# Linear attention and MLP on one core: the first chunk in halves of its heads, and loads and casts of the start moved

## The chip, the cores and the metric

The kernel runs on one core of a Trainium2 chip. The metric is the device time of one execution in microseconds (us). The engines are TensorE (PE; its weight loads are PEld), VectorE (DVE), ScalarE (ACT), GpSimd (POOL) and SyncE (SP), which here issues the loads. Each works through its own instructions in order and waits for the others by semaphores.

## The reference

Eight batches, eight heads, 576 positions, head size 64. First a linear attention, then an MLP over its output:

```
phi(x) = where(x > 0, x, exp(x) - 1) + 1
kv  = einsum(bhsd,bhse->bhde)(phi(k), v);  z = sum_s phi(k)
x   = einsum(bhsd,bhde->bhse)(phi(q), kv) / (phi(q) . z + 1e-6)   -> [4608, 512]
out = gelu_tanh(x @ w_in) @ w_out          w_in [512, 2048], w_out [2048, 512]
```

All inputs and the output are float32; the kernel multiplies in bfloat16.

## The kernel before

Everything is written out in program order by hand (`manual_schedule`); the order in the Python code is the order of each engine's instructions. The MLP runs in nine iterations (`iteration(j)`): iteration j takes the first 512 positions of batch j as four chunks of 128 tokens, and the ninth takes what is left of all batches. In an iteration h = x @ w_in is made in 16 blocks of 128 columns (`h_ps`, one PSUM bank each, four matmuls of 512 tokens, line 349), ACT applies GELU to each (line 359), and the second product (`o_ps`, line 650) accumulates over the 16 blocks for the four chunks. Work for later batches is hung onto the steps of an iteration by number with `at(j, slot, fn)`; in iteration 0 slots 0 to 15 are the h blocks and slots 16 to 31 are the groups of four o matmuls, in the order u (four blocks of w_out each) and, within it, chunk t.

PSUM is used as two pools: six single banks (`bank`, tag b) and one pair of banks (`pair_of_banks`). The loads of q, k, v, w_in and w_out share seven SBUF buffers (`pld`), and SP issues them in the order of the code: q and k of batch 0 in alternating halves, v in halves, four blocks of w_in (1 MB each), then w_out blocks between the loads of batch 1. Each w block is cast from float32 to bfloat16 by `cast_w_in` (line 137) or `cast_w_out` (line 143), which take the engine as an argument.

`first_batch` has nothing to overlap with. It makes phi of q and k (lines 212, 223, 236), transposes q on PE (line 395), casts v (line 241), makes kv in two halves `ii` (line 263; half ii gives the head pairs, or blocks, ii and 2+ii) and puts it as blocks into `kvbd` (line 290). `keep_warm(n)` issues n matmuls of zeros (line 385). Then for each chunk c: `nab` multiplies q by the four blocks (`n_ps`, line 294, in the pair of banks; `nab_in_banks` uses two single banks and evacuates them one by one), DVE divides (a reciprocal, lines 307 and 329, and a product, lines 309 and 330) into x; `transpose_x` transposes x by four PE matmuls into one bank (line 341), which ACT copies into xt (line 342). `h_quarter(0, c, 3)` computes h blocks 0 to 2 for that chunk alone, contracting over the four blocks of x's columns. Iteration 0 then goes on with the GELUs and blocks 3 to 15.

`plan_second` is the attention of batch 1, placed into iteration 0: `maps` (exp, linear part, minimum; slot 15), `transpose_q` (23), `casts` of v (25), `kv` and `last_w_out` (26), then `n` and `t` for the chunks (27 to 31). `gelu_table()` loads ACT's table with GELU; the exps need another table, and the framework inserts that load itself. Copies on ACT need neither.

Of the kernel before, what the change touches and what calls it, by code (L numbers as in the profile page):

```python
# [8 lines left out]
FP32 = mybir.dt.float32  # L9
BF16 = mybir.dt.bfloat16  # L10
# [5 lines left out]
def kernel(  # L16
# [57 lines left out]
    def bank(name, shape, dt=FP32):  # L74
        return ps_b.tile(shape, dt, name=name, tag="b")
# [51 lines left out]

    w_st = {}

    def load_w(wr, i):  # L130
        t = pld.tile([P, 4, 512], FP32, name="w_st", tag="ld")
        w_st[wr is w_in_r, i] = t
        src = wr[:, :, 512 * i : 512 * (i + 1)] if wr is w_in_r else wr[:, 4 * i : 4 * i + 4, :]
        nc.sync.dma_start(out=t, in_=src)

    def cast_w_in(i, fn, fs=slice(0, 512)):
        fn(
            out=w_in_sb[:, :, 512 * i + fs.start : 512 * i + fs.stop],
            in_=w_st[True, i][:, :, fs],
        )  # L140

    def cast_w_out(i, fn, ms=slice(0, 4)):
        fn(
            out=w_out_sb[:, 4 * i + ms.start : 4 * i + ms.stop, :],
            in_=w_st[False, i][:, ms],
        )
# [8 lines left out]
    for s in range(2):  # L155
        load_pairs("v", v, 0, halves[s])
    for i in range(4):
        load_w(w_in_r, i)
    load_w(w_out_r, 0)
    ld_tile("q", 1)  # L160
    load_q_paired(1)
# [95 lines left out]
    def kv_paired(b, ii, kv_of):  # L257
        kp, vp = phi["k", b], vp_paired(b)
        for j in range(J):
            for s in range(2):  # L260
                for a in range(2):
                    r, u = slice(HP * a, HP * (a + 1)), 2 * ii + s
                    nc.tensor.matmul(  # L263
                        kv_of(a, ii)[HP * s : HP * (s + 1)],
                        lhsT=kp[r, j, u, :],
                        rhs=vp[r, j, u, :],
                        start=(j == 0),
                        stop=(j == J - 1),
                        skip_group_check=True,
                    )  # L270
# [16 lines left out]
    def kv_evac(b, blocks, src, fn):  # L287
        for s in range(2):
            r = slice(HP * s, HP * (s + 1))
            fn(out=kvbds[b % 4][r, blocks, E * s : E * (s + 1)], in_=src[r])  # L290
# [44 lines left out]
            )  # L335
        return x

    def transpose_x(x, xt_c, fn):
        t_ps = bank("t_ps", [P, NP, P], BF16)
        for i in range(NP):  # L340
            nc.tensor.transpose(t_ps[:, i, :], x[:, P * i : P * (i + 1)], ident)  # L341
        fn(out=xt_c, in_=t_ps)

    xts = {}
    qts = {}

    def h_mm(h_ps, xt, m, ts=slice(0, MAIN)):
        for c in range(KM):
            nc.tensor.matmul(  # L349
                h_ps[:, ts],  # L350
                lhsT=w_in_sb[:, c, P * m : P * (m + 1)],
                rhs=xt[:, c, ts],
                start=(c == 0),
                stop=(c == KM - 1),
                skip_group_check=True,
            )
# [3 lines left out]

    h_begun = {0: {}, 1: {}}

    def h_begin(j, m, ts):
        if m not in h_begun[j]:
            h_begun[j][m] = bank("h_ps", [P, MAIN])
        h_mm(h_begun[j][m], xts[j], m, ts)

    def h_quarter(j, c, blocks):
        for m in range(blocks):
            h_begin(j, m, slice(P * c, P * (c + 1)))  # L370

    def xt_chunk(j, c):
        return xts[j][:, :, P * c : P * (c + 1)]
# [1 line left out]
    def gelu_table():  # L375
        nc.scalar.preload_act_table_set("gelu_apprx_tanh_and_others")  # L376
# [3 lines left out]
    def first_batch():  # L380
        w_ps = bank("w_ps", [P, 512])

        def keep_warm(n):
            for _ in range(n):
                nc.tensor.matmul(w_ps, lhsT=warm[:, 0:P], rhs=warm)  # L385

        qt = pt.tile([P, C, NP, P], BF16, name="qt")
        qs = (slice(0, 4), slice(4, 8))

        def transpose_q(s, fn):  # L390
            t_ps = bank("t_ps", [P, C, 2, P], BF16)
            for i in range(2):
                for c in range(C):
                    h = 4 * s + 2 * i
                    nc.tensor.transpose(
                        t_ps[:, c, i, :], phi["q", 0][:, c, h : h + 2, :], ident
                    )
            fn(out=qt[:, :, 2 * s : 2 * s + 2, :], in_=t_ps)

        keep_warm(18)  # L400
        for s in range(2):
            for n, hs in (("q", qs[s]), ("k", halves[s])):
                exp_of(n, 0, hs)
                linear_of(n, 0, hs)
                least_of(n, 0, hs)
        transpose_q(0, nc.scalar.copy)
        keep_warm(10)
        transpose_q(1, nc.scalar.copy)
        keep_warm(2)
        for ii in range(2):  # L410
            cast_v_paired(0, halves[ii], nc.vector.tensor_copy)
        for ii in range(2):
            kv_ps = [bank("kv_ps", [P, E]) for _ in range(2)]
            kv_paired(0, ii, lambda a, ii: kv_ps[a])
            for a, fn in enumerate((nc.vector.tensor_copy, nc.scalar.copy)):
                block = slice(2 * a + ii, 2 * a + ii + 1)
                kv_evac(0, block, kv_ps[a].rearrange("p (i e) -> p i e", i=1), fn)
        gelu_table()
        for s in range(2):
            cast_w_in(0, nc.gpsimd.tensor_copy, slice(256 * s, 256 * s + 256))  # L420
        for i in range(1, 4):
            cast_w_in(i, nc.gpsimd.tensor_copy)
        for i in range(2):
            cast_w_out(i, nc.gpsimd.tensor_copy)
        cast_w_out(2, nc.gpsimd.tensor_copy, slice(0, 2))
        keep_warm(2)

        xts[0] = pt.tile([P, NP, MAIN], BF16, name="xt")
        x = {0: nab(qt[:, 0], 0), 1: nab_in_banks(qt[:, 1], 0)}
        for c in range(C):  # L430
            transpose_x(x[c], xt_chunk(0, c), nc.scalar.copy)
            if c + 2 < C:
                x[c + 2] = (nab, nab_in_banks)[c % 2](qt[:, c + 2], 0)
            if c > 0:
                h_quarter(0, c - 1, 3)
        h_quarter(0, C - 1, 3)

    first_batch()

# [14 lines left out]
    def plan_second():  # L454
        b = 1
        x = {}

        def maps():
            for n in "qk":
                exp_of(n, b)  # L460
            gelu_table()
            for n in "qk":
                linear_of(n, b)
            least_of("q", b)
            cast_w_out(2, nc.vector.tensor_copy, slice(2, 4))
            least_of("k", b)

        def transpose_q():
            qts[b] = pt.tile([P, C, NP, P], BF16, name="qt")
            for s in range(2):  # L470
                t_ps = bank("t_ps", [P, 2, NP, P], BF16)
                for c in range(2):
                    for i in range(NP):
                        nc.tensor.transpose(  # L474
                            t_ps[:, c, i, :],
                            phi["q", b][:, 2 * s + c, 2 * i : 2 * i + 2, :],
                            ident,
                        )
                nc.scalar.copy(qts[b][:, 2 * s : 2 * s + 2], t_ps)

        def casts():
            cast_v_paired(b, halves[0], nc.vector.tensor_copy)
            cast_v_paired(b, halves[1], nc.gpsimd.tensor_copy)

        def kv():
            kv_ps = [bank("kv_ps", [P, 2, E]) for _ in range(2)]
            for ii in range(2):
                kv_paired(b, ii, lambda a, ii: kv_ps[a][:, ii, :])
            for a, fn in enumerate((nc.vector.tensor_copy, nc.scalar.copy)):
                kv_evac(b, slice(2 * a, 2 * a + 2), kv_ps[a], fn)  # L490

        def last_w_out():
            cast_w_out(3, nc.vector.tensor_copy, slice(0, 1))
            cast_w_out(3, nc.scalar.copy, slice(1, 2))
            cast_w_out(3, nc.gpsimd.tensor_copy, slice(2, 4))

        def n(c):
            x[c] = (nab_in_banks if c == 1 else nab)(qts[b][:, c], b)

        def t(c):  # L500
            if c == 0:
                xts[b] = pt.tile([P, NP, MAIN], BF16, name="xt")
            transpose_x(x[c], xt_chunk(b, c), nc.scalar.copy)

        at(0, 15, maps)
        at(0, 23, transpose_q)
        at(0, 25, casts)
        at(0, 26, kv)
        at(0, 26, last_w_out)
        at(0, 27, n, 0)  # L510
        at(0, 27, n, 1)
        at(0, 28, n, 2)
        at(0, 29, t, 0)
        at(0, 29.5, t, 1)
        at(0, 30, n, 3)
        at(0, 30.5, t, 2)
        at(0, 31, t, 3)
        at(0, 31, h_begin, b, 0, slice(0, 3 * P))
        at(0, 31, h_begin, b, 0, slice(3 * P, MAIN))

# [233 lines left out]
```

## Time and profile before

| | us |
|---|---|
| median of five runs | 287.19 |
| lowest and highest run | 287.1, 287.39 |
| profiled execution | 287.2 |
| its span in the trace | 285.4 |
| PE busy | 279.3 |
| ACT, DVE, POOL busy | 163.8, 107.8, 20.3 |

The profile shows one execution, in us from the start of its span. A line of a timeline gives start, duration, engine, line of the kernel, operation, output<-inputs, shapes and count; in brackets the idle time before it and what ended it. A line of the waits gives the total, how often, and the longest. A busy engine off the chain that ended last costs nothing by itself. TensorE's granted clock is 1.0 throughout.

### The profile page before, as it was taken

How to read it: one execution, taken by the hardware profiler on the slowest of the kernel's cores; microseconds unless marked ns; L12 is line 12 of the kernel's file. 1: busy time of each engine (PE TensorE's matmuls, PEld its weight loads, DVE VectorE, ACT ScalarE, POOL GpSimd, SP SyncE). 2: the span in 40 equal slices, each digit the busy share in tenths (PEclk: the TensorE clock that was granted, in tenths of full speed). 3: DMA queues.
4: the chain of work that ended last, by engine and by line, in shares of the span. 5: the costliest groups of instructions: out<-in, count | busy, mean ns of one | idle time of the engine just before them, and what ended most of it. 6: DMA issues, size and time to landing. Idle time of an engine off the chain costs nothing.

```text
span 285.4 us, 4570 instructions
## 1 busy us (share of the span) xinstructions
PE 279.3 (98%) x1864; PEld 136.9 (48%) x1864; DVE 107.8 (38%) x182; ACT 163.8 (57%) x226; POOL 20.3 (7%) x26
## 2 busy tenths in 40 slices
PE   8989999999999999999999999999999999999995
PEld 2564455445454445544554455444544444444444
DVE  3840468534855473543246614640412010000001
ACT  4866866795966935683458635763572275026400
POOL 6066260000000000000000000000000000000000
PEclk9999999999999999999999999999999999999999
DMA  7999999966989948935799479435141230120022
GB/s 252 409 406 398 410 400 273 351 235 200 141 231 328 259 132 240 331 75 144 196 299 229 125 211 362 78 106 153 37 39 45 88 53 0 52 86 11 0 74 74
DMA packets 71539, 53.76 MB, mean 188 GB/s; under 512 B 42080, under 2 KB 62944, under 8 KB 71520
## 3 DMA queue, kind: packets, MB, share of 16 engines
q1 hardware_dynamic: 68736, 44.58, 54.9%
q10 hardware_dynamic: 2784, 8.91, 8.8%
q8 instruction: 14, 0.23, 0.3%
q14 instruction: 5, 0.04, 0.0%
HBM read 36.70 MB, written 9.44 MB: 162 GB/s over the span
## 4 chain that ended last, share of the span: by engine, by line
PE 93%; DMA 3%; DVE 1%; SPq 1%; issue 0%; ACTq 0%; ACT 0%; DVEq 0%
PE h_ps L349 44%; PE o_ps L650 43%; PE n_ps L294 3%; DMA v_x<-in_v_dram 3%; PE kv_ps L278 1%; PE t_ps L341 1%; SPq L91 1%; PE kv_ps L263 0%; SPq L96 0%; PE t_ps L474 0%; DVE x L330 0%; DVE vp L241 0%; DVE x L309 0%; PE w_ps L385 0%; ACTq L616 0%
## 5 line engine op out<-in xcount | busy, mean ns | idle before, releaser
L650 PE MATMUL o_ps<-w_out_sb,g 128*128 128x512 bf16 (+2 forms) x608 | 127.5, 368 | 0.0
L349 PE MATMUL h_ps<-xt,w_in_sb 128*128 128x512 bf16 (+1 forms) x552 | 117.6, 363 | 0.0
L359 ACT ACTIVATE g<-h_ps 128x512 bf16<-128x512 f32 x144 | 85.0, 598 | 46.3 <-PE h_ps L349 45.4
L650 PEld LDWEIGHTS <-g 128*128 128x128 bf16 x608 | 57.8, 98 | 64.5
L349 PEld LDWEIGHTS <-w_in_sb 128*128 128x128 bf16 x616 | 56.5, 98 | 59.6 <-issue 0.6
L611 ACT COPY o_sb<-o_ps 128x512 f32<-128x512 f32 (+2 forms) x20 | 11.1, 560 | 60.6 <-PE o_ps L650 53.5
L611 DVE COPY o_sb<-o_ps 128x512 f32<-128x512 f32 (+1 forms) x18 | 12.0, 667 | 69.9 <-PE o_ps L650 69.9
L307 DVE RECIPROCAL r<-n_ps 128x8 f32<-128x8 f32 x33 | 6.8, 207 | 49.2 <-PE n_ps L294 49.1
L309 DVE TENSOR_TENSOR x<-n_ps,r 128x512 bf16<-128x512 f32 x33 | 22.8, 692 | 1.1
L212 ACT ACTIVATE q_e<-q_x 128x2048 bf16<-128x2048 f32 (+1 forms) x9 | 15.5, 1721 | 2.7 <-DMA q_x<-in_q_dram 2.6
L212 ACT ACTIVATE k_e<-k_x 128x2048 bf16<-128x2048 f32 (+2 forms) x9 | 15.8, 1755 | 0.8 <-DMA k_x<-in_k_dram 0.8
L236 DVE TENSOR_TENSOR q_p<-q_p,q_e 128x2048 bf16<-128x2048 bf16 (+1 forms) x9 | 10.0, 1106 | 14.5 <-ACT q_e L212 14.3
L223 DVE TENSOR_SCALAR q_p<-q_x 128x2048 bf16<-128x2048 f32 (+1 forms) x9 | 9.9, 1101 | 14.0 <-DMA q_x<-in_q_dram 14.0
L349 PE MATMUL h_ps<-xt_rest,w_in_sb 128*128 128x512 bf16 x64 | 14.0, 379 | 0.0
L294 PEld LDWEIGHTS <-qt 128*128 128x128 bf16 x128 | 9.7, 98 | 6.9 <-DVE x L309 0.4
L294 PE MATMUL n_ps<-kvbd,qt 128*128 128x130 bf16 x128 | 12.5, 221 | 0.0
L223 DVE TENSOR_SCALAR k_p<-k_x 128x2048 bf16<-128x2048 f32 (+2 forms) x9 | 10.2, 1133 | 5.3 <-DMA k_x<-in_k_dram 5.3
L385 PE MATMUL w_ps<-warm 128*128 128x512 bf16 x32 | 10.5, 492 | 1.2 <-DVE warm L177 1.2
L236 DVE TENSOR_TENSOR k_p<-k_p,k_e 128x2048 bf16<-128x2048 bf16 (+2 forms) x9 | 11.1, 1228 | 0.9 <-ACT k_e L212 0.7
L290 DVE CAST kvbd<-kv_ps 64x260 bf16<-64x260 f32 (+2 forms) x18 | 6.6, 366 | 10.8 <-PE kv_ps L278 8.3
L376 ACT ACT_TABLE_LOAD x8 | 10.3, 1283 | 0.1
L212 ACT ACT_TABLE_LOAD x8 | 10.3, 1283 | 0.1
(49 smaller groups left out, 97.0 us busy)
## 6 DMA issues: line engine op xcount, KB each, us to landing
out_dram<-o_sb ACTq DMA_DIRECT2D x16, 512.0 KB, 3.2
q_x<-in_q_dram SPq DMA_DIRECT2D x6, 1024.0 KB, 7.2
k_x<-in_k_dram SPq DMA_DIRECT2D x6, 1024.0 KB, 11.2
v_x<-in_v_dram SPq DMA_DIRECT2D x6, 1024.0 KB, 6.6
w_st<-in_moe_w_in_dram SPq DMA_DIRECT2D x4, 1024.0 KB, 14.5
w_st<-in_moe_w_out_dram SPq DMA_DIRECT2D x4, 1024.0 KB, 13.6
q_x<-in_q_dram SPq DMA_DIRECT2D x4, 512.0 KB, 8.5
k_x<-in_k_dram SPq DMA_DIRECT2D x2, 576.0 KB, 5.5
```

The costliest lines, as they stand in the source:

```text
L212: nc.scalar.activation(by_chunk(exps[name, b], hs), x[:, hs].rearrange("p h (c d) -> p h c d", d=D), AF.Exp,)
L223: nc.vector.tensor_scalar(by_chunk(phi[name, b], hs), x[:, hs].rearrange("p h (c d) -> p h c d", d=D), 1.0, 1.0, op0=ALU.add, op1=ALU.max,)
L236: nc.vector.tensor_tensor(p, p, e, op=ALU.min)
L294: nc.tensor.matmul(ns[i // 2][rows, 2 * E * (i % 2) : 2 * E * (i % 2 + 1)], lhsT=qt_c[:, i, rows], rhs=kvbd[:, i, :], skip_group_check=True,)
L307: nc.vector.reciprocal(r, n_v[:, :, :, D])
L309: nc.vector.tensor_tensor(x_view(x, paired), n_v[:, :, :, 0:D], r[:, :, :, None].to_broadcast([P, 2, NP, D]), op=ALU.mult,)
L349: nc.tensor.matmul(h_ps[:, ts], lhsT=w_in_sb[:, c, P * m : P * (m + 1)], rhs=xt[:, c, ts], start=(c == 0), stop=(c == KM - 1), skip_group_ ...
L359: nc.scalar.activation(g[:, m, :], h_ps, AF.Gelu_apprx_tanh)
L376: nc.scalar.preload_act_table_set("gelu_apprx_tanh_and_others")
L385: nc.tensor.matmul(w_ps, lhsT=warm[:, 0:P], rhs=warm)
L611: (nc.scalar.copy if on_scalar else nc.vector.tensor_copy)(dst, src)
L650: nc.tensor.matmul(o_ps, lhsT=g[:, m, P * t : P * (t + 1)], rhs=w_out_sb[:, m, fs], start=(m == 0), stop=(m == MM - 1),)
```

## The change

In `first_batch` the first chunk is made in two halves of its heads (`nab_half`): two matmuls, reciprocal, product, two transposes, a copy of two blocks of xt; h blocks 0 and 1 of that chunk are contracted over two blocks of columns at a time. h blocks 0 to 3 instead of 0 to 2 are made in quarters (block 3's first two chunks in one go), in an order written out by hand. The second half of kv goes into the pair of banks and ACT alone copies it out; one of two warm matmuls behind it is left out. Chunk 2 instead of 1 and 3 uses two single banks. The first w_in block is loaded in two halves of its columns, and POOL casts it as 128, 128 and 256 columns; the first half of w_in's second block is cast by DVE, after x of chunk 3. The table load for GELU moves from behind kv to behind the last xt copy. In batch 1 it moves from behind the exps (slot 15) to behind ACT's cast of w_out (slot 26); DVE and POOL swap their halves of w_out's third block; and the second half of v is cast by ACT instead of POOL.

```diff
-    def load_w(wr, i):
+    def load_w(wr, i, parts=1):
...
-        nc.sync.dma_start(out=t, in_=src)
+        for fs in (slice(0, 256), slice(256, 512)) if parts == 2 else (slice(0, 512),):
+            nc.sync.dma_start(out=t[:, :, fs], in_=src[:, :, fs])
...
-        load_w(w_in_r, i)
+        load_w(w_in_r, i, 2 if i == 0 else 1)
...
+    def nab_half(x, qt_c, ii):
+        n_ps = bank("n_ps", [P, 4 * E])
+        for a in range(2):
+            nc.tensor.matmul(
+                n_ps[:, 2 * E * a : 2 * E * (a + 1)],
+                lhsT=qt_c[:, 2 * a + ii, :],
+                rhs=kvbds[0][:, 2 * a + ii, :],
+                skip_group_check=True,
+            )
+        n_v = n_ps.rearrange("p (a s e) -> p a s e", a=2, e=E)
+        r = psm.tile([P, 2, 2], FP32, name="r2")
+        nc.vector.reciprocal(r, n_v[:, :, :, D])
+        nc.vector.tensor_tensor(
+            x[:, 4 * D * ii : 4 * D * (ii + 1)].rearrange("p (s a d) -> p a s d", a=2, d=D),
+            n_v[:, :, :, 0:D],
+            r[:, :, :, None].to_broadcast([P, 2, 2, D]),
+            op=ALU.mult,
+        )
...
-        for ii in range(2):
-            kv_ps = [bank("kv_ps", [P, E]) for _ in range(2)]
-            kv_paired(0, ii, lambda a, ii: kv_ps[a])
-            for a, fn in enumerate((nc.vector.tensor_copy, nc.scalar.copy)):
-                block = slice(2 * a + ii, 2 * a + ii + 1)
-                kv_evac(0, block, kv_ps[a].rearrange("p (i e) -> p i e", i=1), fn)
-        gelu_table()
-        for s in range(2):
-            cast_w_in(0, nc.gpsimd.tensor_copy, slice(256 * s, 256 * s + 256))
-        for i in range(1, 4):
+        kv_ps = [bank("kv_ps", [P, E]) for _ in range(2)]
+        kv_paired(0, 0, lambda a, ii: kv_ps[a])
+        for a, fn in enumerate((nc.vector.tensor_copy, nc.scalar.copy)):
+            kv_evac(0, slice(2 * a, 2 * a + 1), kv_ps[a].rearrange("p (i e) -> p i e", i=1), fn)
+        kv_ps = pair_of_banks("kv_ps")
+        kv_paired(0, 1, lambda a, ii: kv_ps[:, a, 0:E])
+        kv_evac(0, slice(1, 4, 2), kv_ps[:, :, 0:E], nc.scalar.copy)
+        for fs in (slice(0, 128), slice(128, 256), slice(256, 512)):
+            cast_w_in(0, nc.gpsimd.tensor_copy, fs)
+        cast_w_in(1, nc.gpsimd.tensor_copy, slice(256, 512))
+        for i in range(2, 4):
             cast_w_in(i, nc.gpsimd.tensor_copy)
         for i in range(2):
             cast_w_out(i, nc.gpsimd.tensor_copy)
-        cast_w_out(2, nc.gpsimd.tensor_copy, slice(0, 2))
-        keep_warm(2)
+        cast_w_out(2, nc.gpsimd.tensor_copy, slice(2, 4))
+        keep_warm(1)
...
+        nab_half(x[0], qt[:, 0], 0)
+        nab_half(x[0], qt[:, 0], 1)
+        x[1] = nab(qt[:, 1], 0)
+        t(0, first)
+        t(0, second)
+        for m in range(2):
+            h(m, 0, 1, first)
+        x[2] = nab_in_banks(qt[:, 2], 0)
+        for m in range(2):
+            h(m, 0, 1, second)
+        t(1)
+        x[3] = nab(qt[:, 3], 0)
+        cast_w_in(1, nc.vector.tensor_copy, slice(0, 256))
+        h(2, 0)
+        h(0, 1)
+        t(2)
+        h(1, 1)
+        h(2, 1)
+        h(3, 0, 2)
+        h(0, 2)
+        t(3)
+        gelu_table()
+        for m in range(1, 4):
+            h(m, 2)
+        for m in range(4):
+            h(m, 3)
...
         def maps():
             for n in "qk":
                 exp_of(n, b)
-            gelu_table()
...
-            cast_w_out(2, nc.vector.tensor_copy, slice(2, 4))
+            cast_w_out(2, nc.vector.tensor_copy, slice(0, 2))
...
-            cast_v_paired(b, halves[1], nc.gpsimd.tensor_copy)
+            cast_v_paired(b, halves[1], nc.scalar.copy)
...
             cast_w_out(3, nc.scalar.copy, slice(1, 2))
+            gelu_table()
             cast_w_out(3, nc.gpsimd.tensor_copy, slice(2, 4))
```

Here `h(m, c, n, blocks)` computes h block m for n chunks from chunk c on, over the given blocks of columns, and `t(c, blocks)` is `transpose_x` for the given blocks.

More of the change, by code (lines that the diff above doesn't have):

```diff
@@ L336, in nab_in_banks, with transpose_x, h_mm @@
         return x
[L338 to L342, printed above, removed]
+    def nab_half(x, qt_c, ii):
[16 more added lines that the diff above has]
+        )
+    def transpose_x(x, xt_c, fn, blocks=range(NP)):
+        t_ps = bank("t_ps", [P, len(blocks), P], BF16)
+        for n, i in enumerate(blocks):
+            nc.tensor.transpose(t_ps[:, n, :], x[:, P * i : P * (i + 1)], ident)
+        fn(out=xt_c[:, blocks.start : blocks.stop], in_=t_ps)
     xts = {}
     qts = {}
-    def h_mm(h_ps, xt, m, ts=slice(0, MAIN)):
-        for c in range(KM):
+    def h_mm(h_ps, xt, m, ts=slice(0, MAIN), blocks=range(KM)):
+        for c in blocks:
             nc.tensor.matmul(
@@ L361, with h_begin @@
     h_begun = {0: {}, 1: {}}
-    def h_begin(j, m, ts):
+    def h_begin(j, m, ts, blocks=range(KM)):
         if m not in h_begun[j]:
             h_begun[j][m] = bank("h_ps", [P, MAIN])
[L366 to L370, printed above, removed]
+        h_mm(h_begun[j][m], xts[j], m, ts, blocks)
     def xt_chunk(j, c):
@@ L424, in first_batch, with t, h @@
             cast_w_out(i, nc.gpsimd.tensor_copy)
-        cast_w_out(2, nc.gpsimd.tensor_copy, slice(0, 2))
-        keep_warm(2)
+        cast_w_out(2, nc.gpsimd.tensor_copy, slice(2, 4))
+        keep_warm(1)
         xts[0] = pt.tile([P, NP, MAIN], BF16, name="xt")
[L429 to L436, printed above, removed]
+        x = {0: px.tile([P, d_model], BF16, name="x")}
+        def t(c, blocks=range(NP)):
+            transpose_x(x[c], xt_chunk(0, c), nc.scalar.copy, blocks)
+        def h(m, c, n=1, blocks=range(KM)):
+            h_begin(0, m, slice(P * c, P * (c + n)), blocks)
+        first, second = range(2), range(2, 4)
+        nab_half(x[0], qt[:, 0], 0)
[24 more added lines that the diff above has]
+            h(m, 3)
     first_batch()
```

## The prediction

> **What bounds the kernel now.** I read the page first, then the waits of TensorE (PE), then the timeline of the first 64 us, since the edits touch batches 0 and 1 only.
>
> ```profile
> span 285.4 us, 4570 instructions
> PE 279.3 (98%) x1864; PEld 136.9 (48%) x1864; DVE 107.8 (38%) x182; ACT 163.8 (57%) x226; POOL 20.3 (7%) x26
> PE 93%; DMA 3%; DVE 1%; SPq 1%; issue 0%; ACTq 0%; ACT 0%; DVEq 0%
> ```
>
> PE is busy for 98% of the span and carries 93% of the chain that ended last. No engine but PE can be worth much, and PE only where it stands still. The waits of PE are four:
>
> ```profile
> PE w_ps L385 <- DVE warm L177: 1.2, 1, 1.2
> PE t_ps L341 <- DVE x L309: 0.8, 1, 0.8
> PE t_ps L341 <- DVE x L330: 0.5, 1, 0.5
> PE kv_ps L263 <- DVE vp L241: 0.3, 1, 0.3
> ```
>
> The second and third, 1.27 us, lie in the stage that the change rebuilds. Its timeline:
>
> ```profile
> 12.36 0.48 PE L263 MATMUL kv_ps<-vp,k_p 64*64 64x65 bf16 x36 [0.26 <-DVE vp L241]
> 12.77 0.60 PE L385 MATMUL w_ps<-warm 128*128 128x512 bf16 x2
> 12.92 0.43 ACT L290 CAST kvbd<-kv_ps 64x65 bf16<-64x65 f32 x2 [0.24 <-PE kv_ps L263]
> 13.37 1.28 ACT L376 ACT_TABLE_LOAD   x1
> 14.02 0.69 DVE L309 TENSOR_TENSOR x<-n_ps,r 128x512 bf16<-128x512 f32 x1
> 14.77 0.40 PE L341 MATMUL t_ps<-ident,x 128*128 128x128 bf16 x4 [0.80 <-DVE x L309]
> 15.20 0.58 ACT L342 COPY xt<-t_ps 128x512 bf16<-128x512 bf16 x1 [0.55 <-PE t_ps L341]
> 18.14 1.89 POOL L137 CAST w_in_sb<-w_st 128x2048 bf16<-128x2048 f32 x1 [1.92 <-DMA w_st<-in_moe_w_in_dram]
> ```
>
> From 13.78 to 17.74 VectorE (DVE) makes the four x without a gap, so DVE paces this stage. From 16.3 PE is continuous to its end. What the change gains is how much earlier h block 4 starts, if nothing later hits a landing. Before, the fourth quarters start at 18.95 (copy of the last xt ends at 18.90); 12 quarter matmuls (0.67) and block 3 (0.865) put block 4 at 20.49.
>
> **The change, part by part: the first batch.** Durations of that execution: a 128-column matmul issues every 0.056 us; its result is usable 0.22 us after its start (four took 0.40). A 128x4 reciprocal with a 128x256 product repeats after 0.54 us (15.18 to 15.72), a full pair after 0.85 (15.72 to 16.57). A copy of xt costs 0.585; of 256 columns, by the slope to the 1.003 of 1024 columns, 0.38 (bounds 0.21 of a 64x65 cast and 0.585). PE follows 0.05 us behind DVE or ACT.
>
> One warm matmul is removed: PE is free at 12.99, not 13.21. The first half's two matmuls need only blocks 0 and 2, copied out by 12.68, so DVE starts at 13.30 instead of 13.78. The second kv half now goes out by two ACT casts of 64x130, 0.54 (their row at 42.25), for 0.43 before: ready at 13.46, covered by DVE's first half, which ends at 13.93. DVE then ends: second half 14.48, x1 15.33, x2 16.43, x3 17.28. That is 0.46 earlier; the work is as long as before (0.54 + 0.54 against one 0.85, while x3 is one full pair, 0.85, instead of two halves), so only the start moves.
>
> PE: first two transposes 13.99, ACT copy 14.30 to 14.67; second two 14.54, copy 14.85 to 15.22. Blocks 0 and 1 on the first half 14.72; x2's matmuls 14.94; second half 15.27; t(1) 15.49, its copy 15.91 to 16.50; x3's matmuls 15.71; h(2,0) 15.93; then a wait to 16.55; h(0,1), t(2) 16.77, copy to 17.77; h(1,1), h(2,1) 16.99; four 256-column matmuls of block 3, 0.44, 17.43; h(0,2) 17.87; t(3) 18.09, copy 18.51 to 19.10; three quarters to 18.98; the last four (0.89) 19.15 to 20.04. Block 4 at 20.04: 0.45 us earlier. A check: 16 n, 16 transposes and 16 quarters cost 5.5 us, 12.99 + 5.5 = 18.5, and the waits add about 1.6. The idle does not vanish; it is only rearranged.
>
> **w_in.** The split load adds one SP issue, 0.5 us at 3.9; behind it wait the other w_in issues, whose transfers run 10 us and more behind them, so it costs nothing. Rows of 1 KB instead of 2 KB: the q half (512 KB) took 1.37 us between landings, 383 GB/s, the k half 404, so the split may delay all that follows by 0.13. POOL's casts: 0.52 each for blocks 0 and 1, 1.04 for 2 and 3. Block 0 of the loads landed at 14.1, v at 11.5; the first half should land at 12.8 (bounds 12.8 and 14.2). At 12.9 the blocks are ready at 13.9 and 15.3, needed at 14.72 and 15.93. If both halves land at 14.2, block 1 is late by 0.5 and the gain shrinks to 0.1. I take the early end: the halves of q and k landed 1.4 us apart. w_in 1 landed at 18.14: DVE's half (0.69, its row at 36.44) ends at 18.8, POOL's by 19.7 (a half took 1.04, but 1.56 beside a DVE cast at 36.47); blocks 4 and 6 need them at 20.04 and 21.77. Behind the DVE cast stands nothing until 28.47.
>
> **The table load** moves behind the last xt copy: 19.10 to 20.38. GELU 0 ends at 20.97; its bank is wanted by block 6 at 21.77. ACT then does one GELU per 0.55 us against PE's 0.865 and catches up by block 9. Cost nothing, cover 0.8.
>
> Here a rule speaks against it. "ScalarE: Activation LUTs", section "What ACT_TABLE_LOAD costs", in the Trainium skill, puts a drain of 1.38 us onto a load of 1.283, 2.66 in all. The trace has the 1.283 but no drain behind it (the first two lines below). By the page's figure block 6 would wait 0.6 us and the gain would be gone; I go by the row.
>
> **Batch 1.**
>
> ```profile
> 31.66 1.28 ACT L212 ACT_TABLE_LOAD   x1
> 32.95 1.91 ACT L212 ACTIVATE q_e<-q_x 128x2048 bf16<-128x2048 f32 x1
> 36.47 1.56 POOL L143 CAST w_out_sb<-w_st 128x1024 bf16<-128x1024 f32 x1 [3.59 <-DMA w_st<-in_moe_w_out_dram]
> 39.28 1.76 POOL L241 CAST vp<-v_x 128x1152 bf16<-128x1152 f32 x1 [1.26 <-DMA v_x<-in_v_dram]
> 41.33 0.67 PEld L263 LDWEIGHTS <-k_p 64*64 64x64 bf16 x72 [0.42 <-issue]
> 42.81 0.62 ACT L143 CAST w_out_sb<-w_st 128x512 bf16<-128x512 f32 x1
> 44.44 0.58 ACT L611 COPY o_sb<-o_ps 128x512 f32<-128x512 f32 x1 [1.01 <-PE o_ps L650]
> ```
>
> These moves touch no wait of PE as it stands; they widen margins. With PE earlier by g: the swapped w_out halves are ready at 37.13 (DVE) and 38.03 (POOL), needed at 38.64-g and 39.07-g; unswapped, POOL's 38.03 would have met 38.64-g. The v cast on ACT starts when the qt copies end (40.33-g) and takes 1.16 (exp of the same 128x1152) to 1.76 (POOL's row); I take ACT's own 1.16, so it ends at 41.49-g, and the second kv half needs it at 41.67-g (41.33 and half of the 0.67): margin 0.15, and behind it ACT has only the kv casts at 42.25-g. The load now stands after the w_out cast: 43.43-g to 44.71-g; o_sb's copy, due at 44.44-g, ends at 45.29-g instead of 45.02-g, and its bank or DVE's is wanted by t(0) at 45.44-g: margin 0.1. The load taken out at 36.90 was in idle time. Landings cap g: w_in 2 cast at 22.51, needed 23.95-g; w_out 1 at 32.87 for 34.47-g; w_out 3 lands at 41.84, DVE's cast of it starts at 42.86-g, so g up to about 1.0 passes.
>
> **Sum.** Gain 0.45, of it 0.22 the warm matmul's room and the rest DVE's earlier start. The profiled execution took 287.2 for a span of 285.4 (1.8 around it), and the median is 287.19: 284.95 + 1.8 = 286.75, or -0.16%. This kernel's measurement tells changes from about 0.2%, 0.57 us; I end just inside.
>
> **The rivals.** *More is hidden.* Some 14 links make the sum, each good to 0.03 or 0.05, and only 0.13 less is needed to pass 0.57. If the waits at 15.2, 16.15 and 18.98 (0.11, 0.40, 0.17) close, the gain is 1.1, capped at about 1.0 by w_out 3: 286.2 to 286.6. For it: DVE and ACT overlap neighbours by up to 0.1. Against: x3 still ends only 0.46 earlier.
>
> *w_in late.* Both halves at 14.2, or w_in 1 at 19.5 (it landed 4.0 us after block 0, where its neighbours come 2.5 apart): gain about 0.1, 287.1, still no change.
>
> *Slower: ACT binds batch 1's attention.* The v cast, the w_out cast, the load and o_sb's copy now stand in one queue, with margins of 0.15 and 0.1. If the cast costs POOL's 1.76, PE loses 0.45 and the gain is nil. It decides from an excess of 0.15 and turns the kernel slower by 0.57 once the excess reaches 1.2 us, at 287.8. Against: every ACT row of such shapes is within 0.1 of its neighbours.
>
> **How the numbers follow.** No change 0.46: 0.33 for the forecast, 0.13 for late w_in. Faster 0.37: more is hidden. Slower 0.17: ACT's queue, or w_in later than 20. The range 286.0 to 287.7 takes in the cap of 1.0 and a slight loss beyond 287.19 and leaves out 2 in 10.
>
> **What would show it.** Right: DVE's first reciprocal at 13.3, x3 done near 17.3, block 4 near 20.0, the table load beside quarters, PE without waits from 31 to 48. Wrong: a POOL cast of w_in 0 not before 14, a PE wait on ACT near 41 or 45, or block 4 at 19.6 or earlier.

## The result, and the profile after

The changed kernel takes 287.46 us (median of 25 runs, 287.14 to 288.39), the kernel before 287.22 us (median of 45). The ratio is 1.0011, with a 95% interval from 1.0006 to 1.0017: 0.11% slower, within the 0.2% that counts as no change. Forecast was 0.45 us less, measured 0.24 us more. The profiled execution took 287.36 us for a span of 285.6 us; before, 287.2 for 285.4.

The page of the changed kernel: its span, the busy time of each engine, and the shares of the chain that ended last.

```profile
span 285.6 us, 4585 instructions
PE 278.6 (98%) x1871; PEld 137.2 (48%) x1871; DVE 109.0 (38%) x181; ACT 164.6 (58%) x228; POOL 17.5 (6%) x26
PE 93%; DMA 3%; DVE 1%; SPq 1%; ACT 0%; issue 0%; ACTq 0%; DVEq 0%
```

The bound is the same, TensorE with 93% of the chain. VectorE has 1.2 us more and GpSimd 2.8 less.

The first batch did become shorter. The timeline of the changed kernel's first batch (start, duration, engine, line, operation, and in brackets the idle time before it):

```profile
13.44 0.18 DVE L351 RECIPROCAL r<-n_ps 128x4 f32<-128x4 f32 x1 [0.64 <-PE n_ps L343]
...
16.75 0.69 DVE L310 TENSOR_TENSOR x<-n_ps,r 128x512 bf16<-128x512 f32 x1
...
17.36 1.26 DVE L138 CAST w_in_sb<-w_st 128x1024 bf16<-128x1024 f32 x1
...
18.68 0.58 ACT L363 COPY xt<-t_ps 128x512 bf16<-128x512 bf16 x1 [0.74 <-PE t_ps L362]
```

VectorE starts at 13.44 and ends x3 at 17.44; the last copy of xt ends at 19.26 (forecast 13.30, 17.28 and 19.10: all 0.15 late, with kv's second half 0.12 later than before in this execution, 12.48 against 12.36). The waits of TensorE (total, times, longest):

```profile
PE kv_ps L264 <- DVE vp L242: 1.2, 2, 0.8
PE w_ps L402 <- DVE warm L178: 1.2, 1, 1.2
PE o_ps L695 <- DVE w_out_sb L144: 0.3, 1, 0.3
PE t_ps L362 <- DVE x L352: 0.3, 1, 0.3
PE h_ps L370 <- ACT xt L363: 0.2, 1, 0.2
```

The waits of 0.8 and 0.5 for x became 0.3 for x and 0.2 for xt; a wait of 0.2 for kv's second half (`n_ps`) came in as well. The first o matmul, in the timeline of the kernel before and in that of the changed kernel:

```profile
30.84 1.46 PE L650 MATMUL o_ps<-w_out_sb,g 128*128 128x512 bf16 x6
30.57 1.67 PE L695 MATMUL o_ps<-w_out_sb,g 128*128 128x512 bf16 x7
```

It starts at 30.57 instead of 30.84: 0.27 earlier, or 0.39 counted from the start of kv's second half. But the third line of the waits is new. It stands in batch 1, in the timeline of the changed kernel:

```profile
42.21 1.04 POOL L144 CAST w_out_sb<-w_st 128x1024 bf16<-128x1024 f32 x1 [3.87 <-DMA w_st<-in_moe_w_out_dram]
...
42.59 0.94 DVE L144 CAST w_out_sb<-w_st 128x512 bf16<-128x512 f32 x1
...
43.58 0.59 PE L695 MATMUL o_ps<-w_out_sb,g 128*128 128x512 bf16 x2 [0.31 <-DVE w_out_sb L144]
```

The same place in the timeline of the kernel before:

```profile
41.84 1.04 POOL L143 CAST w_out_sb<-w_st 128x1024 bf16<-128x1024 f32 x1 [0.80 <-DMA w_st<-in_moe_w_out_dram]
...
42.86 0.43 DVE L143 CAST w_out_sb<-w_st 128x512 bf16<-128x512 f32 x1
...
43.38 0.81 PE L650 MATMUL o_ps<-w_out_sb,g 128*128 128x512 bf16 x3
```

Before, GpSimd's cast of w_out's fourth block ends at 42.88, and VectorE's part of the same block begins at 42.86 and takes 0.43. After, the block landed 0.37 later, and VectorE comes 0.27 earlier: its cast begins at 42.59 in the middle of GpSimd's and takes 0.94. The o matmuls behind it start 0.20 later than before instead of 0.27 earlier. From there on the two kernels do the same, and the spans differ by the same 0.2.

### The profile page after: what moved, and what is told of

Read it like the earlier page. It is cut to its first block, busy times and chain, and to the rows that moved or that the text cites. A ratio compares the mean times of both kernels' runs of the same rounds, so it can differ in the third digit from the quotient of the medians.

```text
span 285.6 us, 4585 instructions
## 1 busy us (share of the span) xinstructions
PE 278.6 (98%) x1871; PEld 137.2 (48%) x1871; DVE 109.0 (38%) x181; ACT 164.6 (58%) x228; POOL 17.5 (6%) x26
## 4 chain that ended last, share of the span: by engine, by line
PE 93%; DMA 3%; DVE 1%; SPq 1%; ACT 0%; issue 0%; ACTq 0%; DVEq 0%
PE h_ps L370 44%; PE o_ps L695 43%; DMA v_x<-in_v_dram 3%; PE n_ps L295 3%; PE kv_ps L279 1%; PE t_ps L362 1%; SPq L91 1%; PE kv_ps L264 0%; DVE w_out_sb L144 0%; SPq L96 0%; PE t_ps L518 0%; DVE x L352 0%; DVE vp L242 0%; ACT xt L363 0%; DVE kvbd L291 0%
## 5 line engine op out<-in xcount | busy, mean ns | idle before, releaser
L370 PE MATMUL h_ps<-xt,w_in_sb 128*128 128x512 bf16 (+3 forms) x560 | 118.1, 361 | 0.2 <-ACT xt L363 0.2
L370 PEld LDWEIGHTS <-w_in_sb 128*128 128x128 bf16 x624 | 57.2, 98 | 59.5 <-issue 0.8
L402 PE MATMUL w_ps<-warm 128*128 128x512 bf16 x31 | 9.4, 458 | 1.2 <-DVE warm L178 1.2
L248 DVE CAST vp<-v_x 128x2048 bf16<-128x2048 f32 x6 | 7.4, 1227 | 8.3 <-DMA v_x<-in_v_dram 8.3
```

Of the source, the lines that this page charges most:

```text
L248: fn(out=vp_main(b)[:, :, :, 0:D].rearrange("p c h d -> p h c d"), in_=ld["v", b].rearrange("p h (c d) -> p h c d", d=D),)
L370: nc.tensor.matmul(h_ps[:, ts], lhsT=w_in_sb[:, c, P * m : P * (m + 1)], rhs=xt[:, c, ts], start=(c == 0), stop=(c == KM - 1), skip_group_ ...
```

## The experiments

Each kernel ran in turn with the kernel before on the same chip, 11 or 12 executions against 29 to 35. "Outside" is the time of an execution less its span. "Low clock" counts executions whose mean granted clock was 0.994 or less; the others have 0.997 or more. All are medians in us.

| kernel | time, before | ratio, interval | span, before | outside, before | low clock |
|---|---|---|---|---|---|
| after, first comparison | 287.46, 287.22 | 1.0011, 1.0006 to 1.0017 | 285.5 | 1.90 | 2 of 26 |
| e1 | 287.30, 287.48 | 1.0001, 0.9985 to 1.0017 | 285.4, 285.7 | 1.98, 1.78 | 2 of 11 |
| e2 | 288.02, 287.48 | 1.0033, 1.0014 to 1.0052 | 285.95, 285.7 | 2.00, 1.78 | 4 of 12 |
| e3 | 288.19, 287.48 | 1.0019, 1.0008 to 1.003 | 285.8, 285.7 | 2.12, 1.78 | 3 of 11 |
| e4 | 287.68, 287.48 | 1.0006, 0.9998 to 1.0015 | 285.9, 285.7 | 1.80, 1.78 | 0 of 11 |
| e5 | 286.91, 287.26 | 0.9989, 0.998 to 0.9998 | 285.1, 285.5 | 1.86, 1.77 | 0 of 11 |
| e6 | 287.55, 287.26 | 1.0009, 1.0 to 1.0018 | 285.8, 285.5 | 1.79, 1.77 | 0 of 11 |
| e7 | 287.31, 287.26 | 0.9999, 0.9991 to 1.0008 | 285.5, 285.5 | 1.79, 1.77 | 0 of 11 |
| e8 | 287.31, 287.26 | 1.0001, 0.9992 to 1.001 | 285.5, 285.5 | 1.80, 1.77 | 0 of 11 |
| e9 | 287.56, 287.45 | 1.0013, 1.0003 to 1.0022 | 285.6, 285.7 | 1.95, 1.79 | 2 of 12 |
| e10 | 287.80, 287.45 | 1.0009, 0.9993 to 1.0025 | 285.75, 285.7 | 1.99, 1.79 | 3 of 12 |
| e11 | 287.48, 287.45 | 1.0006, 0.9996 to 1.0016 | 285.3, 285.7 | 2.12, 1.79 | 0 of 11 |
| e12 | 287.27, 287.45 | 1.0001, 0.999 to 1.0012 | 285.4, 285.7 | 1.83, 1.79 | 0 of 11 |
| e13 | 287.59, 287.47 | 1.0019, 1.0 to 1.0038 | 285.8, 285.7 | 1.79, 1.80 | 4 of 12 |
| e14 | 287.32, 287.47 | 0.9998, 0.9988 to 1.0008 | 285.4, 285.7 | 1.92, 1.80 | 0 of 12 |
| e15 | 287.33, 287.47 | 1.0, 0.9991 to 1.0009 | 285.4, 285.7 | 2.06, 1.80 | 0 of 11 |

The kernel before had a low clock in 1 of its 132 executions here, and 1.73 to 1.86 outside its span in every one. In the texts on record T1 is the theory that VectorE's cast of w_out's fourth block collides with GpSimd's, T2 that the block lands late because the first w_in load was split, T3 that ACT's queue in batch 1 is too long.

Two stretches of the profiles, free of when an execution got going, repeat from kernel to kernel to about 0.02 us. From the start of kv's second half to the first o matmul it is 18.48 or 18.49 with the old first batch (before, e4, e7, e8), 18.09 with the new one (after, e1, e6, e9), 17.92 or 17.93 with t(3) earlier as well (e5, e11, e12); with the second warm matmul back it is 18.30 (e14) and 18.13 (e15), 0.21 more each. From the first o matmul to the first one behind `n_ps` that needs w_out's fourth block it is 12.54 before, 13.01 after, 12.87 in e9 (the same kernel as after) and 12.64 in e1, e5, e6 and e11, where VectorE has no part in that block.

**e1, w_out's fourth block without VectorE.** Everything else as in the changed kernel:

```diff
-            cast_w_out(3, nc.vector.tensor_copy, slice(0, 1))
-            cast_w_out(3, nc.scalar.copy, slice(1, 2))
+            cast_w_out(3, nc.scalar.copy, slice(0, 1))
             gelu_table()
-            cast_w_out(3, nc.gpsimd.tensor_copy, slice(2, 4))
+            for m in range(1, 4):
+                cast_w_out(3, nc.gpsimd.tensor_copy, slice(m, m + 1))
```

> The changed kernel, with the last w_out block cast by ACT (first of four parts) and POOL (the other three, one by one), none by DVE. Three theories for the gain that was lost. T1, collision: in the changed kernel DVE's 128x512 cast of w_out ran beside POOL's cast of the same block and took 0.94 us instead of 0.43, and PE waited for it at 43.5. Then PE has no wait there, its o matmuls of u=3 start near 43.1 instead of 43.58, and the time falls by 0.4 to 286.9 to 287.1. T2, landing: the block simply lands too late (42.2 instead of 41.8) since the split load slowed the stream; then PE waits for POOL or ACT instead and the time stays at 287.4. T3, ACT's queue (v cast, table load) holds PE; then ACT's first part comes late too and the time stays or rises.

The timeline of e1:

```profile
42.11 1.73 POOL L144 CAST w_out_sb<-w_st 128x512 bf16<-128x512 f32 x3 [3.88 <-DMA w_st<-in_moe_w_out_dram]
...
43.22 0.21 DVE L308 RECIPROCAL r<-n_ps 128x8 f32<-128x8 f32 x1 [0.52 <-PE n_ps L295]
...
43.35 0.38 PE L695 MATMUL o_ps<-w_out_sb,g 128*128 128x512 bf16 x1
```

The block lands as late as in the changed kernel (42.11), ACT has the same queue, and yet the matmuls go at 43.35 without a wait in the list of waits, 0.23 earlier than after. The span's median is 0.3 below the kernel before. Of the 0.47 that the stretch had grown, 0.37 went with the cast on VectorE; landing and ACT's queue together account for 0.10 at most. The time did not clearly follow: its median is 0.18 lower, but the ratio is 1.0001 (0.9985 to 1.0017), with 0.20 more outside the span and a low clock in 2 of 11.

**e2, the first w_in load unsplit** (`load_w(w_in_r, i)` for all i).

> The changed kernel, with w_in's first block loaded in one piece again. T2 says that the split costs the stream 0.2 to 0.35 us of landing time: w_out 3 lands near 41.9, DVE's cast no longer meets POOL's, and the time falls to 287.0. T1 says: the first casts of w_in come after 14.2 instead of 13.1, the early gain shrinks to about 0.1, the cast of DVE starts about when POOL's ends, and the time is 287.1 to 287.3. T3: no change from 287.45.

It is slower than any of the three theories had it. TensorE now waits 0.3 for GpSimd's cast of w_in in the first batch, which the split takes away, and the stretch to the first o matmul is 18.57, longer than before the change: without the split the first batch gains nothing. The fourth block landed at 42.43, later than with the split (42.21): T2 is wrong. In 4 of 12 executions the clock was low, twice 0.986 or 0.987 with spans of 288.1 and 288.2.

**e3, the first batch changed, batch 1 as before** (swap, v cast and table load undone).

> The changed kernel without its edits in batch 1: the table load back behind the exps, v's second half cast by POOL again, DVE's and POOL's parts of w_out 2 swapped back, no load behind the w_out 3 casts. T1: PE reaches u=3 early all the same and DVE's cast of w_out 3 meets POOL's: the wait near 43.5 stays, time 287.4 or more (POOL's v cast ends at 41.4, its w_out cast follows at the landing). T3: the wait is gone, 286.8 to 287.0.

Inconclusive on the cast: in its profile the clock fell to half from about 14.2 to 17.6, TensorE came to the place late (43.70), and VectorE's cast, at 43.68 and after GpSimd's end at 43.31, took its usual 0.43. It brought up the clock as a second question.

**e4, the kernel before with a longer cast on GpSimd beside VectorE's.** Theory T1 in the old first batch:

```diff
             cast_w_out(3, nc.vector.tensor_copy, slice(0, 1))
-            cast_w_out(3, nc.scalar.copy, slice(1, 2))
-            cast_w_out(3, nc.gpsimd.tensor_copy, slice(2, 4))
+            cast_w_out(3, nc.gpsimd.tensor_copy, slice(1, 4))
```

> The kernel before, with POOL casting three of the four parts of w_out 3 in one instruction (about 1.6 us from the landing at 41.84) instead of two, and ACT none; DVE's part is unchanged. It lays POOL's cast over DVE's without an earlier PE or a later landing. T1: DVE's cast at 42.86 takes 0.8 to 1.0 us instead of 0.43, PE waits 0.3 to 0.5 at 43.5, time 287.5 to 287.7. T2 and T3: DVE's cast stays at 0.43, no wait of PE, 287.2.

The expected 0.8 to 1.0 did not come. The timeline of e4 says why:

```profile
42.00 1.47 POOL L143 CAST w_out_sb<-w_st 128x1536 bf16<-128x1536 f32 x1 [0.81 <-DMA w_st<-in_moe_w_out_dram]
...
43.29 0.45 DVE L143 CAST w_out_sb<-w_st 128x512 bf16<-128x512 f32 x1
```

GpSimd was done at 43.47, only 0.18 after VectorE's start, and VectorE ended at 43.74, 0.27 after GpSimd. The time of 287.68 lies in the range that T1 gave, but the profile has no wait of TensorE for this cast, so it is no evidence for T1, and the 0.2 in the span has no cause shown. What e4 gives is the end of VectorE's cast. Set beside the others, this is the rule of the collision: a 128x512 cast of VectorE ends 0.27 to 0.28 after GpSimd's cast ends, whenever it began. After: 43.25 and 43.53. e9: 0.81 long, ends 0.28 behind. A 128x1024 cast on VectorE, 17.36 to 18.62 in the first fence above, ends 0.54 after GpSimd's cast of 17.04 to 18.08; where it begins first, it takes 0.69 (e1, at 18.28, and it is GpSimd's cast at 18.31 that then takes 1.56). So VectorE seems to do its fixed part at once (0.43 - 0.27 = 0.16; 0.69 - 0.54 = 0.15) and its elements only when GpSimd has finished.

The kernel before already held a third kind of row, in its timeline, beside GpSimd's cast of 36.47 to 38.03:

```profile
37.04 2.19 DVE L236 TENSOR_TENSOR k_p<-k_p,k_e 128x2304 bf16<-128x2304 bf16 x1
```

This product of two SBUF tensors ends 1.20 after GpSimd; in e13, where no cast of GpSimd ran when it began, it takes 1.36. Not every instruction of VectorE takes turns: the products that read n_ps, in PSUM, take 0.69 beside GpSimd's casts of 14.21 to 16.23 and 0.69 at 43.59, with GpSimd idle.

"GPSIMD Engine Reference", its table of specifications, in the Trainium skill, says that GpSimd's SBUF interfaces are shared with VectorE and that they contend when VectorE runs in a two-port mode or has two SBUF inputs. These rows agree that the two contend: 0.94 for 0.43 in the cast, 2.19 for 1.36 in the product. In which mode VectorE ran the casts no row shows.

**e5 and e11, t(3) earlier on top of e1.** The transpose of chunk 3 ahead of the quarters that need nothing of it:

```diff
         h(2, 1)
+        t(3)
         h(3, 0, 2)
         h(0, 2)
-        t(3)
         gelu_table()
```

> The kernel without DVE's cast of w_out 3 (as in the first experiment), and the last chunk's transposes t(3) ahead of the four quarters h(3, 0, 2) and h(0, 2) instead of behind them; x3 ends at 17.44 there and t(3) came at 18.26. Theory A, the order inside batch 0 still costs PE: the copy of the last xt ends at about 18.6 instead of 19.26, the wait before the last quarters goes and PE is 0.15 to 0.25 earlier at 31; the span falls to 285.0. Theory B, DVE's chain alone sets it: t(3) waits for x3, no change, 285.2.

> The version without DVE's cast of w_out 3 and with t(3) earlier, a second time and on another chip: 0.3 to 0.5 below the kernel before (ratio 0.9982 to 0.9992), span 0.4 shorter than before, 0.4 shorter than the changed kernel.

The span's median was 0.4 below the kernel before on both chips. The time was 0.35 lower on one (0.9989) and the same on the other, where 2.12 us instead of 1.79 lay outside the span. The first is the lowest ratio of the study, but only one of two comparisons shows it. The timeline of e5 also shows the next limit, a wait of TensorE in batch 1:

```profile
44.15 0.38 PE L695 MATMUL o_ps<-w_out_sb,g 128*128 128x512 bf16 x1 [0.18 <-POOL w_out_sb L144]
```

With TensorE this early, GpSimd's last cast of the fourth block, which landed at 42.37, comes too late by 0.18 (0.17 in e12). From here the landing counts.

**e6, PE's waits in the first batch filled, and e12, only more warm matmuls ahead of kv.** e6 is e1 with `keep_warm(4)` instead of 2 ahead of kv and four warm matmuls of 256 columns between the steps of the first two chunks; e12 is e5 with the `keep_warm(4)` alone.

> The kernel of the first experiment with the warm matmuls of zeros that the change took out put back in other places: four instead of two ahead of kv, and four of 256 columns in the waits of PE at 13.3, 14.0 and 14.4. Theory C, the clock: in the kernel with batch 0 alone the granted clock fell to 0.5 from 14.6 to 17.7, since PE had been idle for 1.5 of the 3.5 us before; some executions of all kernels with the new batch 0 have a mean clock of 0.994 and spans 0.5 to 1.5 longer. Then here no execution has a clock under 0.998, and the median span is 285.2 or less. Rival: the fillers delay PE and the clock falls all the same: span 285.4 to 285.8.

> That version with four instead of two warm matmuls ahead of kv. Theory C, the clock: PE is busy 0.43 longer before kv in executions that reach full clock early, so no execution shows a clock under 0.997; kv is not delayed, span as the version without, 285.0 to 285.2. Rival: the warm matmuls end behind the first v cast where full clock comes late, and PE, or the last stores, come later: 285.3 and more.

No low clock in either. In e6 the time outside the span was 1.75 to 1.82 in all executions. The gain did not show in the span: both stretches are those of e1, but the chain's end has ACT's queue for the stores at 281.31 for 1.12 in e6 and at 281.50 for 0.52 before (0.51 to 0.53 in every other profile), and I have no cause for that. e12's span of 285.4 lies where its rival put it, not where theory C did.

**e7, only the batch 1 edits, and e8, only the split load, each on the kernel before.**

> The kernel before with the edits of batch 1 alone (table load behind the w_out 3 casts, v's second half cast by ACT, halves of w_out 2 swapped). T1 (collision in DVE's cast of w_out 3): PE is not earlier, DVE's cast still follows POOL's, no loss: 287.2 to 287.5, as the kernel before. T3 (ACT's queue): PE waits near 41 or 45, 287.7 or more. The time outside the span stays at 1.8 if it is batch 0 that lengthens it, and rises to 1.9 to 2.1 if it is these edits.

> The kernel before with w_in's first block loaded in two halves, nothing else. T2: rows of 1 KB slow the stream, w_out 3 lands 0.13 to 0.35 later against the landing of v (30.33 us behind DVE's second v cast in the kernel before), DVE's cast meets POOL's, 287.4 to 287.7. T1: the landing moves by 0.1 at most; DVE's cast starts as POOL's ends, 287.2 to 287.5.

Neither moves anything: ratios 0.9999 and 1.0001, outside 1.79 and 1.80, no low clock. T3 has no cost to explain; the loss needs the rebuilt first batch.

**e9, the changed kernel again, and e10, the changed kernel with t(3) earlier** (VectorE's cast kept).

> The changed kernel as it is, beside the other three on one chip. T1, collision: PE enters the o matmuls 0.2 to 0.4 earlier than the kernel before, DVE's cast of w_out 3 ends 0.27 behind POOL's cast, PE waits for it near 43.5, and the median span is 0 to 0.2 above that of the kernel before; time 287.3 to 287.6.

> The changed kernel with t(3) ahead of h(3, 0, 2) and h(0, 2), DVE's cast of w_out 3 kept. T1, collision: PE comes to the o matmuls another 0.2 earlier, waits 0.2 longer for DVE's cast at 43.5, and the span stays within 0.1 of the changed kernel's: a gain ahead of the cast is worth nothing. If the collision were not what holds PE, the span would be 0.2 shorter, as where the cast is gone.

e9 gave 1.0013, and its profile the collision again: TensorE waits 0.18 for VectorE's cast. In e10 the span's median was 285.75 (285.7 without its three executions at a low clock), no gain on e9's 285.6, where the same edit without VectorE's cast gave 285.3 on the same chip. An earlier TensorE is worth nothing here as long as the casts collide. (e10's profile fell on a low clock and shows no collision, since TensorE came late; the medians carry this.)

**e13 to e15, the warm matmul.** e13 is the kernel before with one warm matmul instead of two behind kv, the one edit `keep_warm(2)` to `keep_warm(1)`. e14 is e1, and e15 is e5, with `keep_warm(2)` put back there.

> Before with one warm matmul instead of two behind kv, nothing else changed. In the kernel before the second of them lies in a wait of PE for VectorE (13.78 to 14.77), so the work on the path is untouched: span 285.4 to 285.7, ratio 0.999 to 1.001 if nothing but work counts. Theory C1 (the missing warm matmul is what lets the granted clock fall and the time outside the span grow): clock at or below 0.994 in about 2 of 11 executions, time outside the span above 1.86 in half of them, ratio 1.0005 to 1.0015. Theory C2 (it comes from the reordered first chunk, not from the warm matmul): clock 0.998 or more in all, time outside the span 1.73 to 1.85 in all, as before.

> The changed kernel with e1's casts of w_out's fourth block (no cast by VectorE beside GpSimd's) and with the second warm matmul behind kv put back. The first chunk's first matmuls can go 0.1 to 0.2 later: span 285.3 to 285.6 against 285.5 to 285.7 before. C1: no execution with the clock at or below 0.994 and the time outside the span at 1.73 to 1.85; ratio 0.998 to 0.9995. C2: both as in e1 (clock low in 2 of 11, time outside the span with a median of 1.95 to 2.0), ratio 1.0 to 1.001.

> e5 (no cast by VectorE beside GpSimd's, the transpose of chunk 3 ahead of the quarters that need nothing of it) with the second warm matmul behind kv put back. Span 285.0 to 285.4 against 285.5 to 285.7. C1: time outside the span 1.73 to 1.85, ratio 0.9975 to 0.999, the fastest kernel of the study. C2: time outside the span with a median of 1.85 to 2.1, ratio 0.999 to 1.0005.

In e13, 4 of 12 executions had a clock of 0.987 or 0.988 and a span of 287.7 to 287.9, 2.1 longer than the rest. By stretch, in e13's profile: its bounds and length, the busy time (and number of instructions) of PE, PEld, DVE, ACT and POOL, the granted clock (PEclk), DMA share and GB/s:

```profile
10.77:14.18 3.41, 1.68 (x80) 1.35 (x81) 2.64 (x8) 2.58 (x7) 0.00 (x0) 1.00 1.05 409
14.18:17.59 3.41, 2.57 (x24) 2.24 (x23) 3.19 (x11) 1.92 (x3) 2.02 (x2) 0.50 1.05 404
17.59:21.01 3.42, 3.42 (x35) 3.42 (x33) 0.56 (x3) 0.97 (x2) 2.12 (x2) 0.50 1.05 407
21.01:24.00 2.99, 2.94 (x30) 1.92 (x29) 0.00 (x0) 2.31 (x6) 2.38 (x2) 1.00 1.05 409
```

The first stretch in the kernel before's profile:

```profile
10.77:14.18 3.41, 2.94 (x93) 1.88 (x90) 2.62 (x8) 2.60 (x6) 0.00 (x0) 1.00 1.05 408
```

TensorE was busy for 1.68 of the 3.41 us, against 2.94, and then ran at half its clock for two stretches of 3.41 us. Of the 1.26 less only some 0.2 is the matmul taken out; the rest is that the warm matmuls ahead of kv ended early in this execution and kv waited 1.15 for v, which in the profile of before it did not. In e4's profile, with both warm matmuls, kv waited 1.06 in the same way; TensorE was busy for 2.00 of this stretch, and the clock stayed. Nor does the share in this stretch decide alone: e9, e11 and e2 had 1.70, 1.70 and 1.65 there and kept the clock (the bounds are those of e13's clock and need not be theirs).

The verdict rests on the counts: a matmul of zeros taken out, 4 of 12 executions against 1 of 132 (0 of 29 beside it on the same chip). With the changed first batch and one warm matmul there (after, e1, e2, e3, e9, e10) 16 of 84 executions had a low clock; with it put back, or more ahead of kv (e6, e12, e14, e15), 0 of 45. But e5 and e11 have one warm matmul and 0 of 22, which I can't explain, so e12 and e15, which are built on them, show nothing, and e6 and e14 are left with 0 of 23. In the old first batch it is shown that the removal lets the clock fall; in the changed one the counts speak for it and do not prove it.

"TensorE: Matmul & The Clock Gate", Part 1, in the Trainium skill, states a free-running window of 3.4 us, a clock of half or full, and a fall after an idle window. Length and ratio agree with these rows. A fall only after an idle window does not: TensorE was busy for 1.68 of 3.41 us in e13 and for 1.82 of 3.41 in e3 in the stretch before the fall.

The time outside the span is another matter. It stays at 1.79 in e13 and is 1.92 and 2.06 in e14 and e15, so the second warm matmul behind kv does not decide it. With the old first batch no execution has more than 1.86 (before, e4, e7, e8, e13); it grows only with the rebuilt one. Yet not always there: e6 has 1.82 at most, and e12, which differs from e11 by two more warm matmuls ahead of kv alone, has 1.83 where e11 has 2.12 on the same chip. So what TensorE does at the start seems to bear on it. No trace shows how, and its cause stays open.

## Why the prediction was wrong

**The first batch was right.** Start of VectorE, its unbroken run of products, the copies and the quarters followed the sum with a shift of 0.15. The gain was 0.27 by the first o matmul, 0.39 from the start of kv's second half (in four profiles alike), for 0.45 forecast; the room of the warm matmul, 0.22 forecast, was 0.21 (e14, e15). The split load cost nothing (e8) and is needed (e2). The first w_in half was cast from 13.13, the second from 14.46. The estimate for a copy of 256 columns, 0.38, met 0.37. w_in 1 came at 17.04 and not at 18.14, so its cast on VectorE ran beside GpSimd's and took 1.26 instead of 0.69; nothing waited for it.

**The table loads were right.** The load follows the last copy and a GELU follows it at once, in the timeline of the changed kernel:

```profile
19.29 1.28 ACT L393 ACT_TABLE_LOAD   x1
...
20.58 4.74 ACT L380 ACTIVATE g<-h_ps 128x512 bf16<-128x512 f32 x9
```

The GELU starts 0.01 after the load. The drain of 1.38 that "ScalarE: Activation LUTs", section "What ACT_TABLE_LOAD costs", of the Trainium skill states would have put it, by an estimate from that figure, at 21.95; no run here shows one. In batch 1 the load runs from 43.18 to 44.46, and the copy of o_sb that was to be late by a margin of 0.1 starts at 44.64 behind TensorE, not behind the load. The v cast on ACT took 1.18, forecast 1.16. (The two margins of that part, put at 0.15 and 0.1, are 0.18 and 0.15 by its own rows; nothing hung on them.) The slower rival, ACT's queue, did not come (e7).

**The step that failed** is the last of the caps in the part on batch 1: "w_out 3 lands at 41.84, DVE's cast of it starts at 42.86-g, so g up to about 1.0 passes". It priced VectorE's cast at 0.43 wherever it would stand, and looked only at the landing. At 42.86-g the cast lies beside GpSimd's, which had ended at 42.88: the casts had no margin. By the rule of e4 the cast ends 0.27 behind GpSimd's, and GpSimd's end hangs on the landing, not on g. With the 0.05 by which TensorE follows, the o matmul can go at 43.20 at the earliest when the block lands at 41.84: by these rows an estimated cap of about 0.2 (43.38 less 43.20), not 1.0. With the landing of the changed kernel, 42.21, the same sum gives 43.57, and 43.58 was measured. Rows that say so were at hand: 1.56 for GpSimd's cast at 36.47 beside a cast by VectorE, against 1.04, and the product of 2.19 behind it. I used the first for GpSimd's half of w_in 1 and did not ask what it meant the other way round. The landing was also taken as a fixed number from one execution; in the profiles it was 41.84 to 42.53, 42.0 in e4, whose loads are those of before. In the profiled pair the stretch became 0.47 longer, 0.27 earlier turned into 0.20 later; 0.37 of it goes with VectorE's cast (e1). Without that cast the span falls by 0.3 (e1, e14) or 0.4 (e5, e11).

**A second term failed: the 1.8 around the span**, carried over as a constant. Its median grew by 0.1 to 0.3 in most kernels with the new first batch. In e9, beside the kernel before on one chip, the span is 0.1 shorter and the time outside 0.16 longer, and the time is 0.11 longer. So the forecast would not have come true without the collision either: in e1, e11, e14 and e15 the span is 0.3 or 0.4 shorter and the ratio of the times 0.9998 to 1.0006. In e11 the time outside took 0.33 of the 0.4. Only e5 kept its gain (0.9989). Why this time grows stays open.

**The clock was not in the sum.** The warm matmul was taken as room to be gained. In the old first batch it also held the clock, and its removal cost 2.1 us in 4 of 12 executions (e13); in the changed one 16 of 84 were 0.3 to 2.4 longer in the span than the others of their kernel, which moves the mean more than the median.

## What to carry to other kernels

When a change lets an engine arrive earlier, look at what it then runs beside, not only at whether its data has landed: a VectorE cast that used to begin as a GpSimd cast ended (42.86 and 42.88 here) has no margin, and can end no earlier than GpSimd's end plus its own elements (0.27 here). A warm matmul may look like waiting time; before one is removed, look at the granted clock of many executions, since one profile can miss the fall. A gain of 0.1% in the span is not yet one in the time.

## What the runs showed of the hardware

- A cast from SBUF on VectorE and one on GpSimd take turns: 0.94 instead of 0.43 when VectorE comes second (it ends 0.27 behind GpSimd for 512 columns, 0.54 for 1024), 1.56 instead of 1.04 when GpSimd does. So does VectorE's product of two SBUF tensors (2.19 instead of 1.36); its products from PSUM do not (0.69 with and without).
- The granted clock can fall to half for one or two stretches of 3.41 us although TensorE was busy for about half of the stretch before (1.68 of 3.41 in e13, 1.82 in e3).
- The time outside the traced span, 1.73 to 1.86 in every execution of the kernel before, went up to 3.2 in kernels with the new first batch (e14), with nothing in the traces to show for it.
